# Reordering the loads of a kernel's start, one PV order and its last store (attention and a gated MLP on one core)

## The chip, the cores and the metric

One core of one Trainium2 chip. The metric is the device time of one execution in microseconds (us), the lower the better. The profile's span is about 1.8 us shorter than the time (1245.2 against 1247.03 in the profiled run of the kernel before), so spans and times are compared each with its own kind.

## The reference

```python
xn = layernorm(x)                                   # x: 2048 x 512
q  = (xn @ wq) in 32 heads of 128
p  = softmax(q @ k_cache.T / sqrt(128))             # 32 heads, 2048 x 2048 each
s  = (p @ v_cache, heads side by side) @ wo
h  = relu(xn @ w1 + b1) ** 2                        # 512 -> 1792
g  = silu(h @ w2 + b2)                              # 1792 -> 512
out = x + s * g
```

All inputs are bf16. Rows are done in four blocks of 512; a block runs over the 32 heads, so there are 128 "heads" in the kernel's sense. A head has 8 steps; a step is a pair of score matmuls (512 columns each), an exponential of 128x1024 on ACT, and, two steps later, eight PV matmuls of 129 columns. Into the steps TensorE is fed the matmuls of the projections and of the MLP.

## The kernel before

All waits are explicit: each instruction names the ones it depends on. Each engine's program, and each engine's queue of DMA issues, runs in the order in which the code emits it. Cut to what the change and the argument touch:

```python
    # x tiles: one on SP's queue, three on ACT's
    ln_load(0, 0)
    for i in range(1, TPB):
        ln_load(0, i, AC)
    fill_k(0)              # SP, DMA transpose of a head's k, 2048x128
    fill_wq(0, AC)
    ...
    fill_v(0); fill_wq(1); fill_wq(2); load_w1(0); fill_k(1); fill_v(1)
    for i in range(1, 4):
        load_w1(i)         # all of w1, ahead of the loads that the steps emit
    ...                    # layer norm, transposes, query projection of the first head
    first_evac(0, 3)       # both on DVE
    first_proj(3)
    first_evac(3, 1)
    tok_b1 = S.emit_dma(GP, partial(_dma_gather, nc, out=b1b[:],       # 1792 elements of 2 bytes
                                    in_=B_b1.rearrange("(c p) -> p c", p=P)), sl_b1)
    tok_b2 = S.emit_dma(GP, ...)                                       # one row to 128 partitions
    t_b1 = E(DV, partial(_copy, out=b1f[:], in_=b1b[:]), deps=[tok_b1])
    ...
    for pi in range(NPAIR):                # 1024 steps
        gen_scores(pi); ...; gen_pv(pi - 2)
        if k == 0:
            fill_wq(g + 3)                 # SP
            fill_k(g + 2)                  # SP
        if k == 1:
            fill_v(g + 2)                  # SP
```

In `gen_pv` the eight matmuls of a step go to two banks of PSUM, `qt // 2`; the first PV of a head waits, bank by bank, until DVE has copied out the head before.

The softmax here doesn't subtract the row's maximum and nothing guards it: scores larger than these inputs give would overflow.

Of the kernel before, what the change touches and what calls it, by code (L numbers as in the profile page):

```python
# [219 lines left out]
def bass_recurrent_scan__mha_block_cached__dense_activation_squared_relu__prompt_kernel(  # L220
# [87 lines left out]
    def bankF(i):  # L308
        return psF[:, i * 512:(i + 1) * 512]
# [32 lines left out]
    def ln_load(j, i, eng=SP):  # L342
        jt = j * TPB + i
        t_xl[jt] = S.emit_dma(
            eng, partial(_dma, out=x_ln[:, i, :], in_=A_x[0, jt * P:(jt + 1) * P, :]), sl_xl[i],
            deps=[t_xn.get(jt - TPB)])
# [60 lines left out]
                  deps=[t_wqfill[0], tok_xT[0][i]], inc=(c == NDC - 1))  # L407
        t_proj[0] = t

    def first_evac(i, n):  # L410
        t_evac[0] = t_bankF[i // 3] = E(
            DV, partial(_copy, out=qt_sb[:, 0, i * P:(i + n) * P],
                        in_=bankF(i // 3)[:, i * P:(i + n) * P]), deps=[t_proj[0]])

    def warm_up(n):
        for _ in range(n):
# [51 lines left out]
    def gen_scores(pi):  # L468
        g, k = divmod(pi, NPR)
        s2, i = pi % 2, g % NSL  # L470
        assert t_kfill[g] is not None and t_evac[g] is not None
        t = None
        for n in range(2):
            tt = 2 * k + n
            t = E(PE, partial(_mm, out=psA[:, s2 * 1024 + n * 512:s2 * 1024 + (n + 1) * 512],
                              lhsT=kT[:, i, tt * P:(tt + 1) * P], rhs=qt_sb[:, g % NQS, :],
                              start=True, stop=True),
                  deps=[t_exp[pi - 2] if pi >= 2 else None, t_kfill[g], t_evac[g]],
                  inc=(n == 1))
        if k == NPR - 1:  # L480
            t_S_last[g] = t
        t_exp[pi] = E(AC, partial(_act, out=pT[:, pi % NPT, :],
                                  in_=psA[:, s2 * 1024:(s2 + 1) * 1024],
                                  func=ACT.Exp, scale=SM_SCALE),
                      deps=[t, t_PV[pi - NPT] if pi >= NPT else None])

    def gen_pv(pi):
        g, k = divmod(pi, NPR)
        i = g % NSL
        last = k == NPR - 1  # L490
        order = [(n, qt) for n in range(2) for qt in range(TPB)]
        if last:
            order = [(n, qt) for b in range(2) for qt in (2 * b, 2 * b + 1) for n in range(2)]
        t_bank = [None, None]
        t = None
        for idx, (n, qt) in enumerate(order):
            tt, b = 2 * k + n, qt // 2
            tt_first = tt == 0
            inc = idx == 7 or (last and idx == 3)
            t = E(PE, partial(_mm_shared, out=psO[:, b, qt % 2, 0:Dh + 1],  # L500
                              lhsT=pT[:, pi % NPT, n * QB + qt * P:n * QB + (qt + 1) * P],
                              rhs=v_sb[:, i, tt, 0:Dh + 1],
                              start=(tt_first and qt % 2 == 0), stop=(tt == NKT - 1)),
                  deps=[t_exp[pi], t_vfill[g], t_ones,
                        t_oev[g - 1][b] if g >= 1 else None], inc=inc)
            if inc:
                t_bank[b] = t
        t_PV[pi] = t
        if last:
            t_PV_last[g] = t  # L510
            s = g % 2
            for b in range(2):
                t_oev[g][b] = E(DV, partial(_copy, out=o_un[:, s, 2 * b:2 * b + 2, 0:Dh + 1],
                                            in_=psO[:, b, :, 0:Dh + 1]),
                                deps=[t_bank[b], t_onorm[g - 2] if g >= 2 else None])
            tr = E(DV, partial(_recip, out=rden[:, s, :], in_=o_un[:, s, :, Dh]),
                   deps=[t_oev[g][0], t_oev[g][1], t_onorm[g - 2] if g >= 2 else None])
            base = rden[:, s, :]
            rb = bass.AP(tensor=base.tensor, offset=base.offset,
                         ap=[list(base.ap[0]), [1, TPB], [0, Dh]])  # L520
            t_onorm[g] = E(DV, partial(_tt, out=o_bf[:, s, :, :], in0=o_un[:, s, :, 0:Dh], in1=rb,
                                       op=ALU.mult),
                           deps=[tr, tok_oT[g - 2] if g >= 2 else None])
# [31 lines left out]
    def at(step, fn):  # L555
        events.setdefault(step, []).append(fn)
# [74 lines left out]
    def job_wo(j, m, qt, c0=0, c1=D):  # L631
        jt = j * TPB + qt
        h0, h1 = CH[j][m]
        nh = h1 - h0
        last = m == len(CH[j]) - 1
        box = [None]

        def mm(n, bank):
            g = j * H + h0 + n
            place, free = (bankF(bank), t_bankF[bank]) if isinstance(bank, int) else bank  # L640
            box[0] = E(PE, partial(_mm, out=place[:, 0:c1 - c0],
                                   lhsT=oT[:, g % NOT, qt * P:(qt + 1) * P],
                                   rhs=wo_all[:, h0 + n, c0:c1], start=(n == 0),
                                   stop=(n == nh - 1)),
                       deps=[tok_wo[(h0 + n) // HC], tok_oT[g], free], inc=(n == nh - 1))

        def evac(bank, step):
            if qt == TPB - 1:
                for h in range(h0, h1):
                    t_wodone[j * H + h] = box[0]  # L650
            place = (bankF(bank) if isinstance(bank, int) else bank[0])[:, 0:c1 - c0]
            if m == 0:
                t_acc[qt] = t = E(DV, partial(_copy, out=acc[:, qt, :], in_=place),
                                  deps=[box[0], t_fin.get(jt - TPB)])
            elif not last:
                t_acc[qt] = t = E(DV, partial(_tt, out=acc[:, qt, :], in0=place,
                                              in1=acc[:, qt, :], op=ALU.add),
                                  deps=[box[0], t_acc[qt]])
            if m == len(CH[j]) - 2:
                at(step + 1, partial(pre_combine, j, qt))  # L660
            if last:
                s = jt % 2
                t = E(DV, partial(_stt, out=tmp_t[:, s, c0:c1], in0=place, scalar=0.5,
                                  in1=g_all[:, jt % (2 * TPB), c0:c1], op0=ALU.mult,
                                  op1=ALU.mult),
                      deps=[box[0], t_g[jt], t_tmp[s]])
                eng = GP if j == NQB - 1 and qt in (0, 2) else DV
                t_fin[jt] = t_tmp[s] = E(
                    eng, partial(_tt, out=out_t[:, s, c0:c1], in0=tmp_t[:, s, c0:c1],
                                 in1=acc[:, qt, c0:c1], op=ALU.add),  # L670
                    deps=[t, t_u[jt], t_outdma[s]])
                eng, sl = (SP, sl_fin) if j == NQB - 1 else (GP, sl_out)
                dma = S.emit_dma(
                    eng, partial(_dma, out=out[0, jt * P:(jt + 1) * P, c0:c1],
                                 in_=out_t[:, s, c0:c1]), sl[s], deps=[t_fin[jt]])
                if c1 == D:
                    t_outdma[s] = dma
            return t
        return nh, mm, evac
# [63 lines left out]



    m, half = len(CH[-1]) - 1, D // 2
    nt = H - CH[-1][-1][0]
    tail = [job_wo(NQB - 1, m, qt) for qt in range(TPB - 1)]
    tail.append(job_wo(NQB - 1, m, TPB - 1, 0, half))
    tail.append(job_wo(NQB - 1, m, TPB - 1, half, D))  # L750
    n_in, n_after = 14, 22
    n2 = n_in + n_after - 2 * (nt - 1)
    tail_order = [(i, x) for i in range(2) for x in range(nt - 1)] + [(2, x) for x in range(n2)]
    tail_order += [(0, nt - 1), (1, nt - 1)] + [(2, x) for x in range(n2, nt)]
    tail_order += [(i, x) for i in range(3, TPB + 1) for x in range(nt)]
    tail_place = {}

    def tail_one(step):
# [23 lines left out]
            SP, partial(_dma, out=w1_sb[:, :, c0 * P:c1 * P], in_=w1_view[:, :, c0 * P:c1 * P]),  # L782
            sl_w1[i])

    ln_load(0, 0)
    for i in range(1, TPB):
        ln_load(0, i, AC)
    fill_k(0)
    fill_wq(0, AC)
    E(AC, partial(_act, out=th_t[:, 0, 0:1], in_=warm[:, 0:1], func=ACT.Exp), deps=[t_warm])  # L790
# [3 lines left out]
    load_w1(0)  # L794
    fill_k(1)
    fill_v(1)
    for i in range(1, 4):
        load_w1(i)
    for i in range(TPB):
        ln_stats(0, i)  # L800
        if i < 2:
# [14 lines left out]
    first_transpose(3)  # L816
    first_copy(3, DV)
    first_proj(2)
    first_evac(0, 3)
    first_proj(3)  # L820
    first_evac(3, 1)
    tok_b1 = S.emit_dma(GP, partial(_dma_gather, nc, out=b1b[:],
                                    in_=B_b1.rearrange("(c p) -> p c", p=P)), sl_b1)
    tok_b2 = S.emit_dma(GP, partial(_dma, out=b2bc[:],
                                    in_=bass.AP(tensor=B_b2.tensor, offset=B_b2.offset,
                                                ap=[[0, P], [1, D]])), sl_b2)
    t_b1 = E(DV, partial(_copy, out=b1f[:], in_=b1b[:]), deps=[tok_b1])
    tok_w2 = None

    def load_w2():  # L830
# [96 lines left out]
```

## Time and profile before

| | kernel before |
|---|---|
| time, median of 6 runs beside the changed kernel | 1247.01 us (1245.5 to 1248.19) |
| span of the profiled run | 1245.2 us |
| TensorE on the chain that ended last | 97% |
| first score matmul's weights loaded at | 11.18 us |

The view below has the first 20 us in stretches; the columns are stretch, length, PE busy (instructions), granted clock, DMA share, GB/s.

```profile
4.00:8.00 4.00, 3.75 (x20) 1.00 1.32 217
8.00:12.00 4.00, 3.05 (x33) 1.00 1.27 256
12.00:16.00 4.00, 3.96 (x32) 1.00 1.20 203
```

The DMA share is above 1 throughout. The list of DMA issues gives, at the end of each line, the time from issue to landing:

```profile
b2bc<-in_B_b_dram POOLq DMA_DIRECT2D x1, 128.0 KB, 6.3
b1b<-in_B_b_dram POOLq DMA_DIRECT2D x1, 3.5 KB, 7.1
```

### The profile page before, as it was taken

What the parts mean: (1) busy time and instruction counts of PE and PEld (TensorE: products, weight loads), DVE (VectorE), ACT (ScalarE), POOL (GpSimd) and SP (SyncE); (2) the same over time, 40 slices, a digit from 0 to 9 for tenths busy, and PEclk for the clock granted to TensorE, in tenths of its full rate; (3) what the DMA queues carried; (4) which work ended last, traced back from release to release, by engine and by line L of the source; (5) the groups of instructions that cost most, each with busy time, mean ns of one, the idle gap of its engine ahead of it and who ended that gap; (6) DMA issues with size and microseconds to landing.
All of it is one profiled execution on the core that took longest, in us unless ns stands there. A gap on an engine that the chain in (4) does not pass through costs nothing.

```text
span 1245.2 us, 26489 instructions
## 1 busy us (share of the span) xinstructions
PE 1226.2 (98%) x11568; PEld 814.4 (65%) x11776; DVE 471.0 (38%) x946; ACT 1057.1 (85%) x1047; POOL 32.9 (3%) x74
## 2 busy tenths in 40 slices
PE   8999999999999999999999999999999999999998
PEld 4666666666666666666666666666666666666665
DVE  3453332344444333333543533233434333324333
ACT  5888888888888888888888888888888888888885
POOL 1001000000001000000000200000000000000000
PEclk9999999999999999999999999999999999999999
DMA  9999977877787888877887998678778878878861
GB/s 220 219 208 216 170 133 132 145 142 139 130 165 154 154 146 140 144 140 131 144 147 152 170 158 141 132 146 142 135 137 147 150 153 153 141 135 144 145 124 31
DMA packets 686835, 185.39 MB, mean 149 GB/s; under 512 B 675168, under 2 KB 685792, under 8 KB 686720
## 3 DMA queue, kind: packets, MB, share of 16 engines
q1 hardware_dynamic: 684320, 179.36, 79.0%
q0 software_dynamic: 1440, 3.81, 1.2%
q8 instruction: 93, 1.52, 0.5%
q10 hardware_dynamic: 960, 0.52, 0.2%
q14 instruction: 22, 0.18, 0.0%
HBM read 96.08 MB, written 2.10 MB: 79 GB/s over the span
## 4 chain that ended last, share of the span: by engine, by line
PE 97%; SPq 1%; issue 1%; DMA 1%; ACT 0%; DVE 0%
PE psO L157 37%; PE psA L152 35%; PE psF L152 24%; SPq L208 1%; DMA wq_sb<-in_A_wq_dram 1%; SPq L212 1%; ACT pT L161 0%; DVE tmp_t L175 0%; DVE out_t L165 0%
## 5 line engine op out<-in xcount | busy, mean ns | idle before, releaser
L161 ACT ACTIVATE pT<-psA 128x1024 bf16<-128x1024 f32 x1024 | 1045.7, 1024 | 168.6 <-PE psA L152 121.3
L157 PEld LDWEIGHTS psO<-v_sb,pT 128*128 128x128 bf16 x8192 | 549.0, 98 | 244.6 <-issue 14.2
L157 PE MATMUL psO<-v_sb,pT 128*128 128x129 bf16 x8192 | 634.6, 220 | 0.5
L152 PE MATMUL psA<-qt_sb,kT 128*128 128x512 bf16 x1853 | 567.3, 379 | 10.9 <-DVE qt_sb L179 0.7
L179 DVE COPY o_un<-psO 128x258 f32<-128x258 f32 x256 | 97.4, 422 | 406.7 <-PE psO L157 405.9
L152 PE MATMUL psF<-xnT,wq_sb 128*128 128x512 bf16 (+1 forms) x516 | 167.0, 376 | 2.5 <-DMA wq_sb<-in_A_wq_dram 2.2
L152 PE MATMUL psF<-wo_all,oT 128*128 128x512 bf16 x479 | 164.1, 379 | 0.1
L152 PEld LDWEIGHTS psA<-qt_sb,kT 128*128 128x128 bf16 x2048 | 158.3, 98 | 1.4 <-issue 0.6
L179 DVE CAST qt_sb<-psF 128x512 bf16<-128x512 f32 (+1 forms) x129 | 88.4, 686 | 99.6 <-PE psF L152 96.0
L152 PEld LDWEIGHTS psF<-xnT,wq_sb 128*128 128x128 bf16 x524 | 50.8, 98 | 63.4 <-DMA wq_sb<-in_A_wq_dram 2.7
L165 DVE TENSOR_TENSOR o_bf<-o_un,rden 128x512 bf16<-128x512 f32 x128 | 88.6, 692 | 4.6 <-DVE rden L183 0.3
L171 DVE TENSOR_SCALAR r_t<-psF,b1f 128x512 bf16<-128x512 f32 x56 | 42.0, 749 | 113.2 <-PE psF L152 111.3
L152 PEld LDWEIGHTS psF<-wo_all,oT 128*128 128x128 bf16 x480 | 46.9, 98 | 56.4
L152 PE MATMUL psF<-xnT,w_sb 128*128 128x512 bf16 x223 | 77.3, 379 | 0.5 <-DVE qt_sb L179 0.5
L152 PE MATMUL psF<-w_sb,h2T 128*128 128x512 bf16 x221 | 73.0, 379 | 0.0
L152 PEld LDWEIGHTS psF<-xnT,w_sb 128*128 128x128 bf16 x224 | 21.9, 98 | 27.2 <-issue 1.0
L152 PEld LDWEIGHTS psF<-w_sb,h2T 128*128 128x128 bf16 x224 | 21.9, 98 | 26.4
L165 DVE TENSOR_TENSOR z_t<-psF,b2bc 128x512 f32<-128x512 f32 x16 | 11.1, 692 | 65.7 <-PE psF L152 55.6
L165 DVE TENSOR_TENSOR acc<-psF,acc 128x512 f32<-128x512 f32 x28 | 19.3, 689 | 35.9 <-PE psF L152 35.9
L208 POOL DMA_DIRECT2D out_dram<-out_t x12 | 6.7, 556 | 885.3 <-DVE out_t L165 885.3
L165 DVE TENSOR_TENSOR h2T<-r_t 128x512 bf16<-128x512 bf16 x56 | 23.8, 425 | 1.9
L183 DVE RECIPROCAL rden<-o_un 128x4 f32<-128x4 f32 x128 | 22.9, 179 | 4.4
(41 smaller groups left out, 152.2 us busy)
## 6 DMA issues: line engine op xcount, KB each, us to landing
v_sb<-in_A_v_cache_dram SPq DMA_DIRECT2D x128, 512.0 KB, 4.8
wq_sb<-in_A_wq_dram SPq DMA_DIRECT2D x127, 128.0 KB, 3.1
wo_all<-in_A_wo_dram SPq DMA_DIRECT2D x4, 1024.0 KB, 6.4
kT<-in_A_k_cache_dram SPq DMA_TRANSPOSE x128, 4.6
oT<-o_bf SPq DMA_TRANSPOSE x128, 3.9
x_t<-in_A_x_dram POOLq DMA_DIRECT2D x16, 128.0 KB, 3.5
w_sb<-in_B_w_dram SPq DMA_DIRECT2D x1, 1792.0 KB, 10.3
x_ln<-in_A_x_dram SPq DMA_DIRECT2D x13, 128.0 KB, 2.8
```

Of the source, the lines that this page charges most:

```text
L152: return e.matmul(out, lhsT, rhs, start=start, stop=stop)
L157: return e.matmul(out, lhsT, rhs, start=start, stop=stop, skip_group_check=True)
L161: return e.activation(out, in_, func, bias=bias, scale=scale)
L165: return e.tensor_tensor(out, in0, in1, op)
L171: return e.tensor_scalar(out, in0, scalar1=scalar1, scalar2=scalar2, op0=op0, op1=op1)
L179: return e.tensor_copy(out, in_)
L183: return e.reciprocal(out, in_)
L208: return e.dma_start(out, in_)
L212: return e.dma_start(out, in_, transpose=True)
```

## The change

The intent: bring wq of the fourth head ahead of weights that are needed much later, bring the x tiles in sooner, take DVE's long wait for b1 out of the start, drop a wait at each head's start, and make the last store smaller. The diff, cut:

```diff
-    ln_load(0, 0)
-    for i in range(1, TPB):
-        ln_load(0, i, AC)
+    for i in range(TPB):
+        ln_load(0, i, SP if i % 2 == 0 else AC)
 ...
-    for i in range(1, 4):
-        load_w1(i)
+    at(0, partial(load_w1, 1))          # at(step, ...): emitted with the steps
+    at(8, partial(load_w1, 2))
+    at(8, partial(load_w1, 3))
+    tok_b1 = S.emit_dma(GP, partial(_dma_gather, ...), sl_b1)      # moved up, nearly first on GpSimd
+    tok_b2 = S.emit_dma(GP, ...)
+    at(2, bias_f32)                     # the cast of b1, behind the first PV
 ...
-    first_evac(0, 3)
+    first_evac(0, 3, AC)
     first_proj(3)
-    first_evac(3, 1)
-    tok_b1 = ...; tok_b2 = ...
-    t_b1 = E(DV, partial(_copy, out=b1f[:], in_=b1b[:]), deps=[tok_b1])
+    first_evac(3, 1, DV)
 ... in gen_pv
-        if last:
+        if last or k == 0:
             order = [(n, qt) for b in range(2) for qt in (2 * b, 2 * b + 1) for n in range(2)]
 ... at the end
+    cuts = [0, D // 2, 3 * D // 4, D]   # last tile: 256, 128, 128 columns instead of 256, 256
```

More of the change, by code (lines that the diff above doesn't have):

```diff
@@ L408, in first_proj, with first_evac @@
         t_proj[0] = t
-    def first_evac(i, n):
-        t_evac[0] = t_bankF[i // 3] = E(
-            DV, partial(_copy, out=qt_sb[:, 0, i * P:(i + n) * P],
-                        in_=bankF(i // 3)[:, i * P:(i + n) * P]), deps=[t_proj[0]])
+    def first_evac(i, n, eng):
+        out, in_ = qt_sb[:, 0, i * P:(i + n) * P], bankF(i // 3)[:, i * P:(i + n) * P]
+        op = (partial(_act, out=out, in_=in_, func=ACT.Copy) if eng is AC
+              else partial(_copy, out=out, in_=in_))
+        t_bankF[i // 3] = E(eng, op, deps=[t_proj[0]])
     def warm_up(n):
@@ L477, in gen_scores @@
                               start=True, stop=True),
-                  deps=[t_exp[pi - 2] if pi >= 2 else None, t_kfill[g], t_evac[g]],
+                  deps=[t_exp[pi - 2] if pi >= 2 else None, t_kfill[g], t_evac[g],
+                        t_bankF[0] if pi == 0 else None],
                   inc=(n == 1))
@@ L742, in fill_one @@
         return True
-    m, half = len(CH[-1]) - 1, D // 2
+    m = len(CH[-1]) - 1
+    cuts = [0, D // 2, 3 * D // 4, D]
     nt = H - CH[-1][-1][0]
     tail = [job_wo(NQB - 1, m, qt) for qt in range(TPB - 1)]
-    tail.append(job_wo(NQB - 1, m, TPB - 1, 0, half))
-    tail.append(job_wo(NQB - 1, m, TPB - 1, half, D))
+    tail += [job_wo(NQB - 1, m, TPB - 1, c0, c1) for c0, c1 in zip(cuts, cuts[1:])]
     n_in, n_after = 14, 22
@@ L754, in bass_recurrent_scan__mha_block_cached__dense_activation_squared_relu__prompt_kernel @@
     tail_order += [(0, nt - 1), (1, nt - 1)] + [(2, x) for x in range(n2, nt)]
-    tail_order += [(i, x) for i in range(3, TPB + 1) for x in range(nt)]
+    tail_order += [(i, x) for i in range(3, len(tail)) for x in range(nt)]
     tail_place = {}
@@ L796, in bass_recurrent_scan__mha_block_cached__dense_activation_squared_relu__prompt_kernel, with bias_f32 @@
     fill_v(1)
-    for i in range(1, 4):
-        load_w1(i)
+    at(0, partial(load_w1, 1))
+    at(8, partial(load_w1, 2))
+    at(8, partial(load_w1, 3))
+    tok_b1 = S.emit_dma(GP, partial(_dma_gather, nc, out=b1b[:],
+                                    in_=B_b1.rearrange("(c p) -> p c", p=P)), sl_b1)
+    tok_b2 = S.emit_dma(GP, partial(_dma, out=b2bc[:],
+                                    in_=bass.AP(tensor=B_b2.tensor, offset=B_b2.offset,
+                                                ap=[[0, P], [1, D]])), sl_b2)
+    t_b1 = None
+    def bias_f32():
+        nonlocal t_b1
+        t_b1 = E(DV, partial(_copy, out=b1f[:], in_=b1b[:]), deps=[tok_b1])
+    at(2, bias_f32)
     for i in range(TPB):
@@ L818, in bass_recurrent_scan__mha_block_cached__dense_activation_squared_relu__prompt_kernel @@
     first_proj(2)
-    first_evac(0, 3)
+    first_evac(0, 3, AC)
     first_proj(3)
-    first_evac(3, 1)
-    tok_b1 = S.emit_dma(GP, partial(_dma_gather, nc, out=b1b[:],
-                                    in_=B_b1.rearrange("(c p) -> p c", p=P)), sl_b1)
-    tok_b2 = S.emit_dma(GP, partial(_dma, out=b2bc[:],
-                                    in_=bass.AP(tensor=B_b2.tensor, offset=B_b2.offset,
-                                                ap=[[0, P], [1, D]])), sl_b2)
-    t_b1 = E(DV, partial(_copy, out=b1f[:], in_=b1b[:]), deps=[tok_b1])
+    first_evac(3, 1, DV)
+    t_evac[0] = t_bankF[1]
     tok_w2 = None
```

## The prediction

> **What bounds the kernel now.** I read the page first (busy shares, then the chain that ended last), then the windows of the first 34 us, then the timeline of the start, of one head boundary and of the end.
>
> ```profile
> span 1245.2 us, 26489 instructions
> ...
> PE 1226.2 (98%) x11568; PEld 814.4 (65%) x11776; DVE 471.0 (38%) x946; ACT 1057.1 (85%) x1047; POOL 32.9 (3%) x74
> ...
> PE 97%; SPq 1%; issue 1%; DMA 1%; ACT 0%; DVE 0%
> ```
>
> TensorE is the bound: 97% of the chain. Its matmuls are pipelined, so busy time alone proves little; the distance between starts does. In mid-kernel a 512-column matmul follows another every 0.216 us and a group of eight PV matmuls takes 0.45 us, again and again. A change that leaves the number of matmul columns alone can only win what TensorE loses at the start, at the head boundaries and at the end. The start loses most:
>
> ```profile
> 22.00:23.00 1.00, 0.31 (x2) 1.00 2.76 260
> 23.00:24.00 1.00, 0.00 (x0) 1.00 0.07 20
> 24.00:25.00 1.00, 0.50 (x6) 1.00 1.05 239
> 25.00:26.00 1.00, 1.00 (x9) 0.81 0.97 216
> 26.00:27.00 1.00, 1.00 (x8) 0.50 0.92 209
> 27.00:28.00 1.00, 1.00 (x7) 0.50 1.20 255
> 28.00:29.00 1.00, 1.00 (x6) 0.50 1.22 207
> 29.00:30.00 1.00, 0.95 (x11) 0.98 1.05 156
> ```
>
> Columns are stretch, length, PE busy (instructions), granted clock, DMA share, GB/s. PE stands still from 22.3 to 24.5, and then runs at half clock for over 3 us. The timeline names the cause:
>
> ```profile
> 13.19 4.11 SPq L208 DMA_DIRECT2D w_sb<-in_B_w_dram  x3
> ...
> 15.97 0.18 DVE L179 CAST b1f<-b1b 128x14 f32<-128x14 bf16 x1 [4.90 <-DMA b1b<-in_B_b_dram]
> 16.05 1.28 DVE L179 CAST qt_sb<-psF 128x512 bf16<-128x512 f32 x2
> ...
> 16.88 0.59 PE L152 MATMUL psF<-xnT,w_sb 128*128 128x512 bf16 x2 [0.51 <-DVE qt_sb L179]
> ...
> 17.34 0.54 SPq L208 DMA_DIRECT2D wq_sb<-in_A_wq_dram  x1
> ...
> 24.50 0.39 PE L152 MATMUL psF<-xnT,wq_sb 128*128 128x512 bf16 x1 [2.19 <-DMA wq_sb<-in_A_wq_dram]
> ```
>
> The fourth head's wq is issued at 17.34, behind three w1 loads on the same queue, and lands 7.11 us later (the chain's DMA step). And DVE sat 4.90 us on the b1 gather with two finished query tiles behind it in its queue.
>
> **What the Trainium skill says.** "TensorE: Matmul & The Clock Gate", section "What's actually happening": an idle PE falls to half clock, and windows are 3413 ns. The trace agrees on half clock and its length (0.50 for three whole windows); but the page asks for about 3.4 us of idleness, and here 2.2 us were enough. Same page, "Step-by-step: what each phase is for": weight loads are pulled ahead of running matmuls; the trace agrees, each load starts with the matmul before it, so a short wait ahead of a load can be free. "DMA: Bandwidth & Descriptors", "Issuing engines are not separate DMA queues": two queues save issue time only. Here an x load costs 0.4 to 0.46 us of issue (three took 1.38 on ACT), so I count one or two issues for that part, no bandwidth. "SBUF — State Buffer", "Who interferes with whom": a DVE operation with two SBUF inputs and a GpSimd operation exclude each other. The trace agrees at the end: DVE's out_t add of 128x256 takes 0.91 us beside GpSimd's, 0.42 alone.
>
> **The change, part by part.**
>
> (a) w1 parts 1 to 3 leave the queue ahead of wq. The stall: at the pace of 0.216 us the matmul that started at 24.50 was due at 22.15 (the last score matmul started at 21.93), so 2.35 us are lost there. The clock: 3.4 us at half speed lose half, 1.7 us. Without the three w1 loads (0.5 + 0.384 + 0.384 MB, about 5.8 us at the 220 GB/s of the page's first slices) wq is issued right behind the second v load, near 13.5 instead of 17.34. That v load landed at about 18.8 (4.8 us is the median landing time, 6 in this crowd), and I expect wq within a microsecond of it, 19.5 to 20. PE will want it at about 21.1 (22.15 less what (b) and (c) bring). So both go: 4.05 us.
>
> (b) The b1 gather is issued at about 2 us instead of 8.87 and the cast that waits for it moves behind the first PV. At 7.1 us to landing it is there at about 9. The wait of PE at 16.88 was due at 16.21 (15.99 + 0.216), so 0.67 us.
>
> (c) x tiles over two queues, first query eviction on ACT. x tile 3 was third on ACT, behind the start of the k transpose, and its statistics began only at 7.09, though DVE was ready at 6.65. Now it is second. Its chain (statistics, rstd, scale, transpose, copy, projection) ends about 0.3 us sooner, the rest bound by ACT's copies, which do not move. The eviction of 384 columns goes to ACT beside DVE's 128; before, DVE did both in 0.85 us, but the larger one was hidden under the last projection, so this alone brings next to nothing and only keeps pace with the earlier x tile. First scores 11.2 to about 10.85: 0.35 us. k, v and wq on SP slip by one issue, 0.4 us; they have more slack than that, save wq of the second head (landing 10.7, used at 11.86), which I let cost 0 to 0.3.
>
> (d) First PV by bank. One boundary:
>
> ```profile
> 1215.27 0.76 DVE L179 COPY o_un<-psO 128x258 f32<-128x258 f32 x2 [4.28 <-PE psO L157]
> ...
> 1215.82 0.61 PEld L157 LDWEIGHTS psO<-v_sb,pT 128*128 128x128 bf16 x8 [0.20 <-issue]
> 1215.95 0.66 PE L157 MATMUL psO<-v_sb,pT 128*128 128x129 bf16 x8
> ...
> 1216.44 0.59 PE L152 MATMUL psA<-qt_sb,kT 128*128 128x512 bf16 x2
> ...
> 1217.09 0.62 PE L157 MATMUL psO<-v_sb,pT 128*128 128x129 bf16 x8
> ...
> 1217.54 0.59 PE L152 MATMUL psA<-qt_sb,kT 128*128 128x512 bf16 x2
> ```
>
> The first group takes 1216.44 - 1215.95 = 0.49, the next 0.45. The first matmul is not late (the one before started at 1215.73, plus 0.216); the 0.20 ahead of its weights is hidden. The loss is inside: the third matmul opens bank 1, whose eviction ends at 1215.27 + 0.76 = 1216.03 and is seen some 0.05 later, against 1216.06 when it was due. By bank, bank 1 comes fifth, due at 1216.17. The wait vanishes. I count 65 such pieces of 0.49 or 0.50 in the chain in order of time: 65 x 0.041 = 2.7 us. The page's 14.2 us of weight-load waits are not the prize.
>
> (e) Last tile in three. PE work is the same columns (16 x 256 against 32 x 128, at 0.109 and about 0.056). DVE's two operations of the last part: 512 columns took 0.68, 256 took 0.43, so 128 about 0.30: each is 0.13 shorter. But part 1's add ends only at 1241.87, held by GpSimd, and then four operations of 0.30 with gaps of 0.03 are queued: 1243.2, against 1243.14 before. The store is a little smaller. I count 0, within 0.2.
>
> Sum: 4.05 + 0.67 + 0.35 + 2.7 + 0 = 7.8, less 0.3 given back to other waits in the crowded start: 7.5 us, or 0.6% of the time.
>
> **The rivals.** First: DMA is the bound of the start, and the wait moves to the next load. For it: DMA share is at or above 1.0 in almost every slice up to 31 us, and a pause of all traffic fell into 23 to 24 us (20 GB/s) and may fall elsewhere. Against it: the moved 1.27 MB are not used before about step 19, long after, and the first queries' k and v land 3 us or more ahead of use. It would leave a wait of 1 to 2 us, perhaps with the half clock after it: gain only 4 to 5 us, 1243. Second: the head boundary keeps its wait, because bank 0's first load still waits and the margin at the fifth matmul is some 0.03 to 0.09 us. Then the gain is 4.8, time 1242.6. Third, on the good side: the 0.20 waits were worth more than I think, up to 14.2 in all: 1230. The start-to-start distances speak against it. Fourth: ACT becomes the bound. It has 0.29 idle in every step of 1.3 and gets only one short copy more; I give it nothing.
>
> **Range and chances.** 1247.4 - 7.5 = 1239.9. Rival one or two alone gives 1243, better luck with loads or the end 1237; run to run the kernel spreads 2.7 us. Range 1236 to 1244. A 2% gain is 25 us; nothing here holds that much, nor can the parts cost so much: faster 0.01, within 0.98, slower 0.01.
>
> **What would show it.** (a) no PE gap after 20 us, clock 1.00 from the first slice, wq of the fourth head issued near 13.5. (b) b1's cast without a DVE wait, query casts at about 14. (c) first exponential at about 11.5 instead of 11.84. (d) pieces of 0.49 gone, and all first groups of a head at 0.45. (e) the last DVE add ending 1.1 to 1.5 us after the start of the last matmul (before: 1243.14 - 1241.83 = 1.31). It is wrong if a new wait on k, v or wq over 1 us stands in the first 35 us, or if the pieces of 0.49 stay.

## The result, and the profile after

| | before | changed |
|---|---|---|
| median of 6 runs | 1247.01 us | 1248.66 us |
| lowest to highest | 1245.5 to 1248.19 | 1246.23 to 1251.69 |
| span of the profiled run | 1245.2 | 1249.4 |

The ratio is 1.0017, with a 95% interval of 1.0000 to 1.0034. Ratios here are the mean time of one kernel's runs over that of the other's from the same rounds, so not quite the ratio of the medians. The prediction was 1239.9 with a range of 1236 to 1244: missed, and on the wrong side of no change. The page of the changed kernel:

```profile
span 1249.4 us, 26734 instructions
...
PE 98%; DMA 1%; SPq 0%; DVE 0%; issue 0%; DVEq 0%
```

TensorE is still the bound, and the busy shares hardly moved. But the start, in the same stretches as before and one more:

```profile
4.00:8.00 4.00, 3.93 (x21) 1.00 1.36 106
8.00:12.00 4.00, 2.11 (x28) 1.00 1.26 35
12.00:16.00 4.00, 0.00 (x0) 0.51 1.44 43
16.00:20.00 4.00, 0.43 (x2) 0.50 1.12 128
```

Read the last two columns together. The share of the DMA engines is as high as before (1.26 against 1.27 in the second stretch), but they move 35 GB/s instead of 256. The engines are "busy" because packets are open for a long time: a 256-byte packet on SP's queue took 0.14 us on average from 8 to 12 us, and 0.025 us before. A view that shows only the share would hide this. The timeline of the changed kernel names who waits:

```profile
1.65 3.56 SPq L212 DMA_TRANSPOSE kT<-in_A_k_cache_dram  x1
...
1.82 1.33 POOL L217 DMA_DIRECT2D b1b<-in_B_b_dram  x1
...
19.57 1.89 PE L152 MATMUL psA<-qt_sb,kT 128*128 128x512 bf16 x4 [9.22 <-DMA kT<-in_A_k_cache_dram]
```

The first k transpose, issued at 1.65, lands at 19.52 instead of 8.05, and PE waits 9.22 us for it, with the half clock behind the wait. The queries were ready: their eviction ended at 10.68. The two bias loads were held as well (b1 took 7.1 us before, b2 6.3):

```profile
b2bc<-in_B_b_dram POOLq DMA_DIRECT2D x1, 128.0 KB, 16.1
...
b1b<-in_B_b_dram POOLq DMA_DIRECT2D x1, 3.5 KB, 17.1
```

The rest of the change did what it should. At a head's start the timeline of the changed kernel has

```profile
35.60 0.62 PE L157 MATMUL psO<-v_sb,pT 128*128 128x129 bf16 x8
...
36.05 0.59 PE L152 MATMUL psA<-qt_sb,kT 128*128 128x512 bf16 x2
```

0.45 us for the first PV group, where it was 0.49. Cutting the span by when the weights of a score pair are loaded tells where the time went. All values are us, and the last row is a version that comes at the end of the experiments:

| | to first scores | pairs 0 to 8 | 8 to 16 | 16 to 1023 | from 1023 to the end | span |
|---|---|---|---|---|---|---|
| before | 11.18 | 10.48 | 13.48 | 1193.85 | 16.21 | 1245.20 |
| changed | 19.57 | 12.91 | 9.45 | 1191.20 | 16.32 | 1249.45 |
| difference | +8.39 | +2.43 | -4.03 | -2.65 | +0.11 | +4.25 |
| e13, below | 10.74 | 9.81 | 9.45 | 1191.20 | 16.33 | 1237.53 |

The gains of pairs 8 to 16 (the wq gap) and of the head starts are there. 10.8 us lost up to pair 8 (8.39 + 2.43) ate them.

### The profile page after: what moved, and what is told of

Read it like the earlier page. It is cut to its first block, busy times and chain, and to the rows that moved or that the text cites. A ratio compares the mean times of both kernels' runs of the same rounds, so it can differ in the third digit from the quotient of the medians. Undisturbed runs are those within 1.5% of the kernel's fastest.

```text
span 1249.4 us, 26734 instructions
## 1 busy us (share of the span) xinstructions
PE 1235.3 (99%) x11792; PEld 814.3 (65%) x11792; DVE 470.1 (38%) x947; ACT 1056.6 (85%) x1048; POOL 32.7 (3%) x74
## 4 chain that ended last, share of the span: by engine, by line
PE 98%; DMA 1%; SPq 0%; DVE 0%; issue 0%; DVEq 0%
PE psO L157 37%; PE psA L152 36%; PE psF L152 25%; DMA wq_sb<-in_A_wq_dram 1%; SPq L212 0%; DVE out_t L165 0%; SPq L208 0%; DVE tmp_t L175 0%; DVEq L119 0%
## 5 line engine op out<-in xcount | busy, mean ns | idle before, releaser
L161 ACT ACTIVATE pT<-psA 128x1024 bf16<-128x1024 f32 x1024 | 1044.7, 1023 | 172.9 <-PE psA L152 127.3
L152 PE MATMUL psA<-qt_sb,kT 128*128 128x512 bf16 x2048 | 610.5, 380 | 9.2 <-DMA kT<-in_A_k_cache_dram 9.2
L152 PE MATMUL psF<-xnT,wq_sb 128*128 128x512 bf16 (+1 forms) x524 | 169.9, 377 | 0.6 <-DMA wq_sb<-in_A_wq_dram 0.4
```

Of the source, the lines that this page charges most:

```text
L152: return e.matmul(out, lhsT, rhs, start=start, stop=stop)
L161: return e.activation(out, in_, func, bias=bias, scale=scale)
```

## The experiments

Theory A: the two bias loads, now issued early on GpSimd's queue, meet the first k transpose. The first rival: the x tile now on SP ahead of the transpose, or another part, does it.

### Where the loads are issued: e1 and e2

e1 is the changed kernel with both bias loads issued where they were:

```diff
-    tok_b1 = ...; tok_b2 = ...          # early
 ...
     first_evac(3, 1, DV)
+    tok_b1 = ...; tok_b2 = ...
```

> The changed kernel with only the two bias loads on the GpSimd queue moved back to where they were issued before (about 8.3 us); everything else of the change stays. Theory A (the two software-queue loads meet the first k transpose and slow all DMA traffic from 6 to 19 us): the first k lands near 8.5 us as before, the first score matmul starts near 10.9 us, no PE gap over 1 us in the start, and the time is about 1240 us, 0.6% under the kernel before. Rival B (x tiles on SP ahead of the transpose, or anything else of the change in the first 2 us, slows it): the first k still lands after 15 us and the time stays at 1247 to 1250 us. Rival C (the loads stall whichever transpose they meet): the second k transpose, not the first, lands some 10 us late, near 27 us, PE waits there, and the time is 1244 to 1250 us.

Measured: 1241.72 us median against 1245.82, ratio 0.9966 (0.9952 to 0.9979). The first k landed at 7.98, first scores at 10.99. The early place of these loads is what cost most of the gain. One new PE gap of 1.1 us stood at 59.3.

e2 is the kernel before with only that part of the change: the loads early, the cast behind the first PV.

> The kernel before with only the two bias loads issued early and their cast moved behind the first PV; x tiles, w1 order, PV order and tail as before. Theory A: the first k lands near 19 us instead of 8, PE waits about 9 us ahead of the first scores, and, with none of the gains, the time is 1252 to 1258 us. Rival B: first k near 8 us, and the time is about 1246.5 us (only the 0.67 us of the cast won).

Measured: 1246.63 us against 1245.82, ratio 1.0002 (0.9989 to 1.0016). The first k landed at 10.38, not at 19. Theory A in this plain form fell: the early loads alone delay the first k by 2.3 us, and first scores start 0.64 us later than before (11.82). Later PE waits for wq longer than before (2.19), but not at a higher price:

```profile
26.28 0.39 PE L152 MATMUL psF<-xnT,wq_sb 128*128 128x512 bf16 x1 [3.80 <-DMA wq_sb<-in_A_wq_dram]
...
22.00:26.00 4.00, 0.48 (x3) 1.00 1.15 319
26.00:30.00 4.00, 3.67 (x34) 1.00 1.10 245
```

The clock stayed at 1.00 (the two lower lines are stretches of e2), where the kernel before fell to half clock behind its shorter wait, so pairs 8 to 16 took 13.47 us here and 13.48 before. Within the noise the early loads alone cost nothing in all. So they need a partner in the change.

### Which of the two loads: e3 and e4

As e1, but only the b1 gather early (e3), or only the b2 broadcast early (e4).

> The changed kernel with only the b1 gather early (1792 elements of 2 bytes), the b2 broadcast back in its old place. If the tiny elements of the gather are what slows the transposes: first k near 19 us and 1247 to 1251 us. If the 128-fold read of one b2 row in packets of 4096 bytes is: first k near 8.5 us and about 1240 us. If both share it: in between, first k at 11 to 15 us.

> The changed kernel with only the b2 broadcast early, the b1 gather back in its old place. The mirror of the run with the b1 gather early: if the broadcast is what slows the transposes, first k near 19 us and 1247 to 1251 us; if the gather is, first k near 8.5 us and about 1240 us.

e3: 1248.06 us, ratio 1.0016 (1.0002 to 1.0029), first k at 16.54. e4: 1245.21 us, ratio 0.9994 (0.9980 to 1.0007), first k at 10.76, and then a 3.4 us PE gap at 11.5 on the second head's wq, which landed at 15.04, with b1 (14.97). A part of that wait seems to be the gather's, which ran from its old place: its first packet came at 11.90, at the end of the first v, and wq landed 1.5 us behind that v, against 0.6 in e1. This hints that a plain load can be slowed too, by about 1 us. The gather of 3.5 KB is the one that holds the transpose for long. The broadcast is not harmless: it brought the first k 2.8 us later than in e1 (10.76 against 7.98), where its 128 KB at the 217 GB/s of the start would be 0.6 us.

### Partner, queue and element size: e5, e6 and e7

e5 is the changed kernel, bias loads early, with only the x tiles put back (one on SP, three on ACT).

> The changed kernel with only the x tiles put back as before (one on SP, three on ACT); the bias loads stay early. The early bias loads alone delayed the first k by only 2.3 us in the kernel before, so theory A in its plain form is short of a partner. Theory A2 (the x order is the partner: with the third x tile and wq still moving on ACT's queue, the software queue's packets start only after 7 us, when the first k has been read): first k near 10.4 us, first scores near 11.8 us, no 9 us gap, and a time of 1241 to 1243 us. Rival (the partner is elsewhere in the change, or chance from run to run): first k after 15 us and 1247 to 1250 us.

Measured: 1240.47 us against 1247.03, ratio 0.9955 (0.9941 to 0.9970), first k at 9.33. The x order is the partner.

e6 issues both bias loads early, but on ACT's hardware queue behind wq (`emit_dma(AC, ...)`).

> The changed kernel with the two bias loads early, but issued on ACT's hardware queue behind wq instead of GpSimd's software queue. If the software queue is what the transposes suffer from: first k lands by 10 us, no 9 us gap, and about 1240 to 1242 us. If the 2-byte elements as such are, whichever queue carries them: first k after 14 us and 1245 us or more.

Measured: 1240.17 us, ratio 0.9950 (0.9935 to 0.9964), first k at 9.32. The same elements on another queue do no such harm. ACT was held by the issue of b2 for 2.5 us, and first scores started at 11.43.

e7 is e3 with the same bytes taken as rows:

```diff
-                                    in_=B_b1.rearrange("(c p) -> p c", p=P)), sl_b1)
+                                    in_=B_b1.rearrange("(p c) -> p c", p=P)), sl_b1)
```

The bias then sits in the wrong places; the bytes and the queue are those of e3.

> As the run with only the b1 gather early, but the same 3.5 KB read as 128 rows of 28 bytes in place of 1792 elements of 2 bytes (the bias ends up in the wrong places, so the result is wrong on purpose). If the number of tiny elements is the cause: first k by 9 us, no long gap, and about 1240 to 1242 us. If any software-queue load at that moment stalls the transposes: first k near 16 us and about 1247 to 1248 us, as with the gather.

Measured: 1241.05 us, ratio 0.9956 (0.9942 to 0.9970), first k at 7.79. The stretch from 8 to 12 us in e3 (first line) and in e7:

```profile
8.00:12.00 4.00, 2.31 (x31) 1.00 1.26 32
...
8.00:12.00 4.00, 3.33 (x33) 1.00 1.22 257
```

Neither e6 nor e7 escaped by its timing: by the packet records the b1 packets of e7 went out while the first k transpose went from 8% to 53% read, those of e6 from 9% to its end. So it takes the software queue and 2-byte elements together. The trace shows that the queues cut the same 3.5 KB differently: into 32 packets of 96 or 128 bytes on the software queue, 1792 of 2 bytes on ACT's, and 16 of 224 bytes as rows.

One reservation: e5, e6 and e7 ran on one chip, e3 on another, and the changed kernel itself was not run again beside them. That the chip made the difference is not excluded by their times alone; the next section goes by what the traces show of each run.

### Why the x order matters: the place in the transpose

The packet records of the traces answer it. A k transpose is 2048 packets of 256 bytes on SP's queue. Counting those sent when the gather's first packet starts gives its place in the running transpose:

| run | gather's first packet, us | place in the k transpose | that k landed, us |
|---|---|---|---|
| before | 13.94 | second, 98% read | 16.86 |
| changed | 5.46 | first, 37% read | 19.52 |
| e3 | 5.47 | first, 37% | 16.54 |
| e2 | 7.03 | first, all read | 10.38 |
| e5 | 6.19 | first, all read | 9.33 |
| e1 | 12.26 | second, not begun | 17.86 |
| e7 (rows of 28 bytes) | 4.36 | first, 8% | 7.79 |

Where the gather comes in the middle of a transpose, that transpose lands some 8 to 11 us later than in a run without a collision (the first k otherwise near 8 us); where it comes at an end, 1 to 4 us later. Of the small delays not all need be the gather's: in e9 and e10, whose gather came only at 14.8 and 15.7, the first k landed at 8.94 and 9.35. The kernel before was lucky: its gather met the last 2% of the second transpose (the last 3% and 2% in e9 and e10). The x order shifts both: with it the first transpose is issued at 1.65 instead of 1.18 and its first packet goes out at 3.99 instead of 3.21 (changed kernel against e5), while the gather's first packet, issued at the same time, goes out at 5.46 instead of 6.19.

e11 tests this by timing alone: e3 with three small GpSimd operations ahead of the gather.

```diff
+    t_pause = t_idf
+    for _ in range(3):
+        t_pause = E(GP, partial(_ts, out=pause[:], in0=identf[:], scalar1=0.0, scalar2=None,
+                                op0=ALU.is_equal), deps=[t_pause])
     tok_b1 = S.emit_dma(GP, partial(_dma_gather, ...), sl_b1, deps=[t_pause])
```

> As the run with only the b1 gather early (first k at 16.5 us there), but the gather's issue delayed by three small GpSimd operations, from 1.83 to about 3.4 us, so that its packets reach the DMA engines near 7 us instead of 5.5. Theory (the gather only hurts a transpose whose rows are still being read, and the first k has been read by about 7 us): first k lands by 10 us, no long gap, 1240 to 1243 us. Rival (the gather on the software queue hurts beside any transposes queued behind it, whenever it comes): first k, or the wq behind it, comes after 14 us, and the time is 1246 us or more.

Measured: 1241.35 us, ratio 0.9960 (0.9947 to 0.9974). The gather was issued at 3.90, its first packet started at 6.99 with 1995 of 2048 packets read (97%), and the first k landed at 9.87. Issuing the gather 2 us later saved 6.7 us (1248.06 in e3; the two were run on different chips, the kernel before at 1245.82 and 1246.69 there). Nothing else of the start was touched.

### The old place is not safe either: e8 and e14

e8 was meant for the gap at 59.3 us: e1, and besides the x loads of the next rows moved from step 24 to step 42 on SP's queue.

> The changed kernel with the bias loads in their old place, and besides the four x loads of the next block of rows moved two heads later on the SP queue (from step 24 to step 42). In the run without this a new PE gap of 1.1 us appeared at 59.3 us, on a wq that was issued behind those x loads. Theory (the start's gain runs into the pace of SP's queue, and this wait is the part of it that shows): the gap goes and the time falls by about 1 us, to 1240.5 us. Rival (the DMA engines are short of time there, not the queue's order): a gap of the same size shows up at this or the next wq, k or v, and the time stays at 1241.7 us.

Measured: 1244.39 us median, but in two groups: 1241.32, 1240.72 and 1241.42, and 1250.38, 1248.58 and 1247.36. The slow ones have a granted clock of 0.996 or 0.997, as all runs of the changed kernel have (0.995 to 0.997), the others 1.000. The gap at 59 us was gone in the profiled run. As the kernel's code differs from e1 only from step 24 on, and the clock points to a long PE wait, I ran the same kernel again:

> The same kernel as the run with the bias loads in their old place and the x loads later, which spread from 1240.7 to 1250.4 us, beside the one with the software queue unused, on the same chip. Theory (the b1 gather on the software queue meets the second k transpose, and by chance of timing sometimes holds it for long): again two groups, one at 1240 to 1242 us with a clock of 1.00, one at 1246 to 1251 us with a clock of 0.996 or 0.997; and the version without the software queue shows one group only. Rival (that chip's own noise): both kernels spread alike.

Measured: 1248.61 us median. Two runs, 1241.56 and 1243.99, have a clock of 1.000 (the second lies above the group that I had expected). The other four, from 1248.36 to 1253.51, have a clock of 0.995 to 0.997 (the highest lies above its group too). e13, on the same chip, shows one group. The profiled run of e14 caught the slow form. Its stretches:

```profile
12.00:16.00 4.00, 3.96 (x31) 1.00 1.93 146
16.00:20.00 4.00, 2.57 (x23) 1.00 0.65 28
20.00:24.00 4.00, 0.00 (x0) 0.66 1.23 32
```

And from its timeline:

```profile
25.01 0.17 DVE L179 CAST b1f<-b1b 128x14 f32<-128x14 bf16 x1 [10.93 <-DMA b1b<-in_B_b_dram]
...
25.83 1.03 PE L152 MATMUL psF<-xnT,w_sb 128*128 128x512 bf16 x2 [7.21 <-DVE qt_sb L179]
```

It is the same collision one transpose later: the gather's first packet came at 13.29, with the second k half read (51%), and that k landed at 25.56. But the harm reaches PE by another way. PE stood for 7.4 us still within the first head, so not for the second k: it waited for a query cast (qt_sb), which stood in DVE's queue behind the cast of b1, and b1 landed at 24.98. So the cast's new place, behind the first PV, does not take it out of PE's way. In e8's profiled run, one of the lower group, the gather's first packet had come at 12.22, before the second k's first packet. e1's five runs were all in the lower group; e8 and e14, on other chips, were not.

### Single parts on the kernel before: e9, e10 and e15

e9 has only the PV order, e10 only the order of the w1 loads, e15 only the x tiles over both queues; each is the line of the diff above, alone.

> The kernel before with only the order of a head's first PV changed to go bank by bank. Theory of the prediction (65 boundaries lose 0.041 us each in the third matmul): the pieces of 0.49 us go, and the time falls by 2.7 us or 0.2%, to about 1244.3 us; score pairs 64 to 1023 take 1134.5 us instead of 1137.0. Rival (the bank-0 wait ahead of the weight load is what counts and stays): no change, 1246 to 1247 us.

e9: 1244.84 us against 1246.69, ratio 0.9988 (0.9974 to 1.0002): by time alone not clear. By the trace it is: pairs 64 to 1023 take 1134.48 us instead of 1137.00, and the 65 late third matmuls are gone.

> The kernel before with only the three w1 loads moved behind the next k, v and wq. Theory: the PE gap of 2.35 us at 22 us goes, with the 3.4 us of half clock after it, so the time falls by 4 us or 0.3%, to about 1242.8 us. Rival (another load takes its place): a gap of 1 us or more stays between 18 and 40 us, the clock falls all the same, and the time is 1245 us or more.

e10: 1243.35 us, ratio 0.9976 (0.9963 to 0.9990). Pairs 8 to 16 take 9.49 us instead of 13.48, the clock stays at 1.00. First scores started at 12.5 in this run, since the last x tile landed at 8.42.

> The kernel before with only the x tiles spread over both queues. Theory of the prediction: the first scores start at most 0.35 us sooner, a tenth of this reaching the end or not: 1246.3 us. In two runs of kernels with the x tiles as before, the last x tile landed at 8.0 and 8.4 us instead of 7.06, and scores started at 12.1 and 12.5 instead of 11.2. If that is usual, the x order is worth 1 us or more: first scores at 11.0 to 11.3 us in this run, and a time 1 us below the kernel before. If the gap at 22 us (wq of the fourth head) takes it all back, since that wq lands when it lands: no change.

e15: 1247.80 us against 1246.43, ratio 1.0022 (1.0005 to 1.0038), six runs from 1246.35 to 1253.87, clocks down to 0.996. None of the three expected times came: the x order alone makes the kernel slower, by 0.2%. In its profile first scores start at 11.12 us, and the gather, issued 0.5 us earlier than before, meets the second k transpose at its start (that k landed at 19.05 instead of 16.86). A PE gap of 3.0 us at 16.1 is again the wait for query casts behind the cast of b1, which landed at 18.25.

### A version that beats both: e12 and e13

e12 leaves nothing of the biases on the software queue: the b1 gather goes on ACT's hardware queue behind wq, the b2 broadcast on SP's queue at step 10. e13 is e12 with the x loads of the next rows at step 42.

```diff
     fill_wq(0, AC)
+    tok_b1 = S.emit_dma(AC, partial(_dma_gather, ...), sl_b1)
 ...
+    at(10, load_b2)                     # on SP
 ... e13 only
-                at(j * SPB + 3 * NPR, partial(ln_load, j + 1, i))
+                at(j * SPB + 5 * NPR + 2, partial(ln_load, j + 1, i))
```

> The changed kernel with the b1 gather on ACT's hardware queue behind wq, and the b2 broadcast on SP's queue at step 10; nothing of the bias loads is left on the software queue. Theory: first k lands by 9 us and the first scores start at 10.7 to 10.9 us (ACT's queue was held 2.5 us by the b2 load when both were there, and scores started at 11.4), so the time is about 1239.5 us, 0.6% under the kernel before, which was what the prediction said of the change. Rival (something else of the early loads becomes the wait): first scores after 11.4 us or a gap over 1 us up to 60 us, 1240.5 us or more.

e12: 1240.46 us against 1246.69, ratio 0.9953 (0.9941 to 0.9966). First k at 9.41, first scores at 10.74. The gap near 59 us is there, which was the rival's sign; it cost 1.1 us (pairs 16 to 1023 took 1192.29). The waits between 50 and 70 us:

```profile
PE psF L152 <- DMA wq_sb<-in_A_wq_dram: 0.9, 1, 0.9
```

> The version with b1 on ACT's hardware queue and b2 on SP at step 10, and besides the x loads of the next rows two heads later on SP. In that version without this a PE gap of 1.1 us stood at 58.7 us on a wq behind the x loads. Theory (the order of SP's queue): the gap goes and the time falls by 1 us, to about 1239.4 us. Rival (the DMA engines are short of time there): the gap moves to a neighbouring wq, k or v, time unchanged at 1240.5 us.

e13: 1239.66 us against 1246.43, ratio 0.9947 (0.9934 to 0.9960), and its five runs lie within 0.43 us (1239.36 to 1239.79), where the kernel before spreads over 2.8 us on the same chip. The gap is gone, so it was the order of SP's queue: PE, 4 us earlier than before, had reached a wq that the queue still issued behind x loads. The start:

```profile
8.00:12.00 4.00, 3.11 (x33) 1.00 1.30 231
12.00:16.00 4.00, 4.00 (x32) 1.00 1.12 257
16.00:20.00 4.00, 3.95 (x37) 1.00 1.17 202
```

About the same share as in the changed kernel, with six to seven times its GB/s between 8 and 16 us.

## Why the prediction was wrong

Go by its own parts, with e13 against the kernel before in the table of stages, since e13 has all of them and no collision.

- **(a)** w1 behind wq: predicted 4.05 us; pairs 8 to 16 fell by 4.03 in the changed kernel and in e13, by 3.99 in e10. Right against this profile, but the half clock behind the wait, 1.7 us of it, does not seem to come in every execution of the kernel before (3.41 us at half clock lower the mean clock of such a run by 0.0014). Of its 40 runs beside the experiments, 25 have a mean clock of 1.000 and a mean time of 1245.7 us; the other 15 have 0.998 or 0.999 and 1247.4 us. The profiled run (0.999) and the 1247.4 that the prediction started from are of the second kind. e9's profile has the same wait of about 2.2 us without the half clock, and pairs 8 to 16 took 11.81 us there. So (a) is probably worth less than 4.05 on the median.
- **(d)** PV by bank: 2.7 us; pairs 16 to 1023 fell by 2.65. Right. The weight-load waits of 0.2 us stayed (66 of them in e13), as the prediction said of them: not the prize.
- **(e)** last tile: 0; the last stage rose by 0.11 in the changed kernel. DVE's last four operations took 0.29 each. Right.
- **(c)** x tiles and eviction: 0.35; first scores came 0.44 sooner in e13. About right as a gain, against this profile of before. Where the x tile on ACT lands late (8.00 and 8.42 in e9 and e10) it is worth more: first scores came at 12.11 and 12.53 there, at 10.74 in e12 on the same chip. That this part would shift the transpose against the gather was not seen.
- **(b)** is the step that failed, in these words: "The b1 gather is issued at about 2 us instead of 8.87 ... At 7.1 us to landing it is there at about 9." The gain of 0.67 was right (pairs 0 to 8 fell by 0.67 in e13). But the earlier issue was entered as free. The gather landed at 18.93, the first k with it at 19.52: first scores came 8.39 us later, and pairs 0 to 8 took 2.43 us more, partly at half clock. 10.8 us of cost stand in place of 1.0 us of gain from (b) and (c).

e13's span is 7.67 us below that of before, against a sum of 7.8 (7.5 after its allowance), and its time is 1239.66 where 1239.9 was predicted. Some of that agreement is luck: e13 also moves the x loads of the next rows, which the prediction did not have and without which e12's span falls by 6.57 only, and against all runs beside it e13's gain is 0.53%, or 6.6 us. The terms that the prediction had were sized well for the profile that it read; missing were the cost of the early gather and, at 1.1 us, the wq behind x loads at 59 us. Its first rival named the kind, "DMA is the bound of the start, and the wait moves to the next load", but looked at the loads that were moved back and at 1 to 2 us, and not at the one that was moved forward. That rival does fit the gap at 59 us. The profile of before held only a hint of the collision: in the list of DMA issues 3.5 KB took 7.1 us, while the second k transpose was on its way.

What stays open: how a software-queue gather of 2-byte elements holds a transpose. The runs show the three conditions of the long hold (that queue, those elements, a transpose being read), each taken away in a run of its own (e6, e7, e11), but not the mechanism in the DMA engines.

## What to carry to other kernels

A load that is moved earlier is not free because nobody waits for it: ask what is on the DMA engines at its new time, above all for tiny elements beside a DMA transpose. Read DMA share and GB/s together; in these runs a share above 1 at 30 to 45 GB/s, where some 200 are usual, went with a held load. When a change costs and each part alone costs little or nothing, look for the pair: here it took the x order and the early gather together. And compare the granted clock of the single runs before a gain is read from one profile: here 1.7 us of the loss that was to be won back seems to have stood in 15 of 40 runs.

## What the Trainium skill lacked or had wrong

- No page has it; it belongs to "DMA: Bandwidth & Descriptors": a gather of 1792 elements of 2 bytes on GpSimd's software queue that starts while a DMA transpose is being read holds all DMA traffic for 8 to 11 us (35 and 43 GB/s from 8 to 16 us, 256 and 203 before; k landing at 19.52 instead of 8.05). At either end of the transpose it costs 1 to 4 us, as rows of 28 bytes nothing.
- "DMA: Bandwidth & Descriptors", "Issuing engines are not separate DMA queues": issuing from several engines is said to save issue time only. Here the queue decided more than that: the same two bias loads early gave a first k at 19.52 on GpSimd's queue and at 9.32 on ACT's.
- "TensorE: Matmul & The Clock Gate", "What's actually happening": an idle window of about 3.4 us is given for the fall to half clock. In the kernel before 2.2 us of PE waiting were enough (0.50 in one record of 3.41 us, from 25.62 to 29.04). But the length of the wait does not decide it: after waits of 3.8 us in e2 and about 2.2 us in e9 the clock stayed at 1.00. So the prediction's "2.2 us were enough" is no rule; what does decide was not tested.
